# A fused attention and two-layer expert kernel: the matrix engine's order fixed by emission in its middle part, with attention's steps set further apart

## The chip, the cores and the metric

The kernel runs on one core of a Trainium2 chip. A core has five engines with a queue each: TensorE (PE in the profile) for matrix products, VectorE (DVE), ScalarE (ACT), GpSimd (POOL), and SyncE (SP), whose queue here issues every DMA. An engine takes its queue in order; engines wait for each other by semaphores. The metric is the device time of one execution in microseconds, and lower is better.

## The reference

Four batches of eight heads (576 positions, head size 64) go through an attention that adds two parts; its output goes through a gated layer and then a squared-ReLU layer over 2304 tokens.

```
out_d   = softmax(scale * q_d @ k_d.T) @ v_d      # q, k, v averaged over groups of 4 positions
out_loc = softmax(scale * q @ k.T, |i-j| < 4) @ v # a band around the diagonal
x  = repeat(out_d, 4) + out_loc                   # -> (2304, 512)
xn = x / sqrt(mean(x*x) + 1e-6) * rms_g
x  = (silu(xn @ w_gate) * (xn @ w_val)) @ w_out   # 512 -> 1536 -> 512
h  = x @ w_in                                     # 512 -> 2048
out = (s * relu(h)**2 + b) @ w_out2               # 2048 -> 512
```

## The kernel before

Precision comes from splitting each float32 operand into two 16-bit halves and adding three products (high by high, high by low, low by high), so that a product of depth 512 is 12 matmuls in one PSUM tile.

The first layer works on 8 blocks of 288 tokens, two to a batch. `main(blk)` runs `moe1_gv` (12 feature chunks, for each 12 matmuls into `pg`, the gate, and 12 into `pvl`, the value; then the gate's epilogue: tanh on ACT into `u`, two multiplications on DVE, the halves on ACT and POOL) and `moe1_out` (four tiles `po` of 36 matmuls). Both are Python generators that yield after 12 matmuls: this is a **step**. A block has 36 steps. Blocks 0 and 1 run together in `main01`, 48 gate and value steps and then 24 of `po`. `moe1_post` rescales a finished block (its matmuls go into `sn`).

Attention of the next batch is woven in as a side generator, one `next` per step. A batch has four **units** of two heads. Batches 0 and 1 use `early_unit` (float32 transposes on TensorE: tiles `tp`, `tpl`, `tpd`, scores `sl` and `sd`, values `pvd` and `pl`). Batches 2 and 3 use `attn_unit`, whose pieces are, in order:

- load q and k (`qkf`), v (`vd`) and v by windows (`vw`); `vd` and `vw` share one buffer;
- `stats`: squares on ACT, `accb` on POOL, then on TensorE `ss`, from which DVE takes the power of two `sc` to scale by;
- halves of q and k into `qk` (ACT, then DVE), a transposing DMA `qkT<-qk` on SP's queue, and copies into `q_b`;
- `pd` on TensorE from `qk` (the averages), then `qd` and six copies `qd_b`; `sd` on TensorE, softmax, `P_d`, transposing DMA `PdT<-P_d`;
- `sl` on TensorE in two parts, a softmax of each over DVE, ACT and POOL into `P_l`, transposing DMA `PlT<-P_l`;
- halves of the values (`split_v`, on POOL and ACT), then `pvd` and `pl` on TensorE.

`norm` ends a half batch: `ssn`, then `rb` on TensorE. In the kernel before one `yield` stands between two pieces, a unit starts every 10 steps, batch 2 starts with block 2 and batch 3 with block 4. All of this only ranks the instructions: a scheduler with a model of the engines decides at build time in which order each engine's queue holds them, and that order is then fixed on the chip. `tc.high_priority(offset=n)` raises instructions in that ranking.

The weights are fetched and split by another generator, `rest_it` (`prep_gv`, and `weigh` for `w_out`, whose last steps scale the 12 chunks of `w_out`). From block 6 on attention's memory is given to `w_in`, prepared by `prep_in`. The second layer (`ph`, `y`) follows.

Of the kernel before, what the change touches and what calls it, by code (L numbers as in the profile page):

```python
# [8 lines left out]
F32 = mybir.dt.float32  # L9
# [19 lines left out]
GR = 96  # L29
# [3 lines left out]
NJ = 9  # L33
NPART = 4
FP = F1 // NPART
UNIT_STEP = 10
UNIT_STEP0 = 2
UNIT_STEP1 = 4
REST0 = 12
# [32 lines left out]
def kernel(  # L72
# [160 lines left out]
    def load_unit(b, hp, qkf, vd, vw):  # L233
        h0 = 2 * hp
        for t, src in enumerate((q, k)):
            for h in range(2):
                sp.dma_start(out=qkf[:, t, :, h, :], in_=src[b, h0 + h].rearrange("(c p) d -> p c d", p=GR))
        sp.dma_start(out=vd.rearrange("p a r d -> p a (r d)"),
                     in_=v[b, h0:h0 + 2].rearrange("h (t p r) d -> p (h t) (r d)", p=72, r=4))
        sp.dma_start(out=vw[:, :, 0, :], in_=v[b, h0:h0 + 2, 0:WIN, :].rearrange("h p d -> p h d"))  # L240
# [11 lines left out]
        return vs  # L252

    def stats(hp, qkf, vd, junk):
        acc = accs[hp % 2]
        act.activation(out=junk[:, :1536], in_=qkf.rearrange("p t c h d -> p (t c h d)"), func=AF.Square,
                       accum_out=acc[:GR, 0:1])
        act.activation(out=junk[:72, :1024], in_=vd.rearrange("p a r d -> p (a r d)"), func=AF.Square,
                       accum_out=acc[:72, 1:2])
        accb = ap.tile([128, 2], BF16, tag="accb", name="accb")  # L260
        pool.tensor_single_scalar(out=accb, in_=acc, scalar=TINY, op=ALU.add)
        vs = sum4(vd)
        ss = pX.tile([128, 2], F32, tag="x", name="ss")
        pe.matmul(out=ss, lhsT=ones_b, rhs=accb, start=True, stop=True)
        sc, iv = pow2(ap, ss, 2, 13, "sq", 2)
        cs = ap.tile([128, 2], F32, tag="cs", name="cs", bufs=2)
        mul(cs[:, 0:1], iv[:, 0:1], 1.0 / 8, iv[:, 0:1])
        dve.tensor_single_scalar(out=cs[:, 1:2], in_=iv[:, 1:2], scalar=2.0 ** -14, op=ALU.mult)
        return vs, sc, cs

    def softmax_d(sd, scale, de=None):
        dm = ap.tile([128, 3], F32, tag="dm", name="dm", bufs=2)
        dz = ap.tile([128, 3], F32, tag="dz", name="dz", bufs=2)
        dve.tensor_reduce(out=dm, in_=sd, axis=AX.X, op=ALU.max)
        dve.tensor_scalar(out=dm, in0=dm, scalar1=scale, scalar2=-1.0, op0=ALU.mult, op1=ALU.mult)
        if de is None:
            de = ap.tile([128, 3, SD], F32, tag="de", name="de")
        for o in range(3):
            act.activation(out=de[:, o], in_=sd[:, o], func=AF.Exp, bias=dm[:, o:o + 1], scale=scale,
                           accum_out=dz[:, o:o + 1])  # L280
        return de, dz

    def scores_d(qd, cs):
        sd = pX.tile([128, 3, SD], F32, tag="x", name="sd")
# [219 lines left out]
    def attn_unit(b, hp, sq_sum):  # L504
        mp = b <= MASKB
        qkf = ap.tile([GR, 2, 6, 2, D], F32, tag="qkf", name="qkf")
        vd = ap.tile([72, 4, 4, D], F32, tag="vd", name="vd")
        vw = ap.tile([WIN, 2, NJ, D], F32, tag="vd", name="vw")
        load_unit(b, hp, qkf, vd, vw)
        yield  # L510
        qk = ap.tile([GR, 24, 128], F16, tag="qk", name="qk")
        vs, sc, cs = stats(hp, qkf, vd, qk.bitcast(BF16).rearrange("p a b -> p (a b)"))
        yield
        qkv = qkf.rearrange("p t c h d -> p t (c h d)")
        qv = qk.rearrange("p (t l c) x -> p t l (c x)", t=2, l=2)
# [34 lines left out]
        yield  # L550
        for js in JS:
            sl = scores_l([q_b[:, 9 * l:9 * l + 9] for l in range(2)], [kT[:, l] for l in range(2)], js, mp)
            yield
# [6 lines left out]
        sp.dma_start_transpose(out=PlT, in_=P_l.rearrange("p a b -> p (a b)"))  # L560
        vh = ap.tile([WIN, 2, 2, NJ, D], F16, tag="vh", name="vh")
        vdh = ap.tile([72, 2, 4, D], F16, tag="vdh", name="vdh")
        split_v(vs, vw, vdh, vh, sc)
        yield
        od = values_d(vdh, PdT, cs[:, 1:2])
        yield
        for js in JS:
            values_l(b, hp, js, vh, PlT, od, cs[:, 1:2])
            yield
        for hh in range(2):  # L570
            squares(b, hp, hh, sq_sum)
        yield

    def norm(b, hh, sq_sum):
        ss = pX.tile([GR, 3], F32, tag="x", name="ssn")
        for c in range(3):
            cc = 3 * hh + c
# [12 lines left out]
        yield  # L590
        rb = pX.tile([128, TB], F32, tag="x", name="rb")
        for c in range(3):
            for i in range(3):
# [13 lines left out]
        yield  # L607


    ring = [W1[:, 15744 + 1024 * i:15744 + 1024 * i + 1024].bitcast(I32).rearrange("p (n t) -> p n t", t=2)  # L610
# [93 lines left out]
    def moe1_gv(blk, g16, fcs=range(NF1)):  # L704
        for fc in fcs:
# [80 lines left out]

    def attn_batch(b):
        sq_sum = ap.tile([128, S], F32, tag="sqsum", name="sqsum")
        if b == EARLY:
            clear()  # L790
        gens = [(early_unit if b < EARLY else attn_unit)(b, hp, sq_sum) for hp in range(NP)]
        step = UNIT_STEP if b >= EARLY else UNIT_STEP1 if b else UNIT_STEP0
        live = []
        n = halves_ = 0
        while gens or live:
            if gens and n % step == 0:
                live.append(gens.pop(0))
            for g in list(live):
                got = next(g, 0)
                if got == 0:  # L800
                    live.remove(g)
                elif got == "half":
                    halves_ += 1
                    if halves_ == NP:
# [85 lines left out]
    def drain(it):  # L890
        for _ in it:
            pass

    W2 = C2 = None
    for blk in range(NB):
        if blk == NB - 2:
# [30 lines left out]
        for n, ev_ in enumerate(main(blk) if blk else main01()):
            if blk == 0:
                if n % RESTN == 0:
                    for _ in range(REST):  # L930
                        if steps[0] < 12 * NPART + NF1:
                            next(rest_it, None)
            if n == 1 or ev_ == "post":
# [125 lines left out]
```

## Time and profile before

| | |
|---|---|
| median of 3 runs | 1069.01 us (1065.67 to 1071.11) |
| the profiled execution | 1066.8 us, of which the profile's span is 1065.1 us |
| mean granted TensorE clock | 0.971 of full speed |
| busy: TensorE, VectorE, ScalarE, GpSimd | 988.2, 597.1, 517.0, 323.9 us |

Busy time is the time in which an engine has an instruction under way; TensorE's clock has two levels, 1.2 and 2.4 GHz, and a mean of 0.95 over a stretch is a tenth of it at the lower one. In rows of the trace the first number is the start in microseconds from the span's beginning, the second the length, and a bracket at the end gives the time that the engine stood idle just ahead, with what ended it. L716 is line 716 of the kernel.

### The profile page before, as it was taken

The page shows a single profiled execution, that of the slowest core. Times are in us where ns is not written, and L with a number is a line of the kernel's source. Part 1 is how long each engine was busy: PE and PEld are TensorE (multiplying, and loading weights), DVE is VectorE, ACT ScalarE, POOL GpSimd, SP SyncE. Part 2 cuts the span into 40 slices and gives each one's busy share as a digit, 9 for nine tenths or more (in the row PEclk, how much of TensorE's full clock was granted, in tenths as well). Part 3 has the DMA queues.
Part 4 walks back from the last instruction along what each step waited for, and adds up shares of the span by engine and source line. Part 5 has one row for each costly group of instructions (what it writes and reads, how often), then busy time and mean ns, then how long its engine had stood idle before and what let it go on. Part 6 is the DMA issues. An engine that isn't in the chain of part 4 may idle for free.

```text
span 1065.1 us, 20448 instructions
## 1 busy us (share of the span) xinstructions
PE 988.2 (93%) x8198; PEld 668.0 (63%) x8198; DVE 597.1 (56%) x1263; ACT 517.0 (49%) x1174; POOL 323.9 (30%) x417
## 2 busy tenths in 40 slices
PE   7975999999997799888899899999999999999998
PEld 4753777778765677666687677654555545455553
DVE  4798975363884764867826777574332414233240
ACT  3876686355644544555436777663321404132140
POOL 7433753245644355535542206420000000000000
PEclk9986999999988899999999999999999999999999
DMA  9985144010345430555312424300000000000000
GB/s 193 232 223 153 61 134 124 14 24 14 69 83 117 95 62 2 93 103 100 61 24 86 153 86 161 111 1 10 21 10 20 1 30 1 20 11 10 20 1 30
DMA packets 128111, 73.59 MB, mean 69 GB/s; under 512 B 111376, under 2 KB 115984, under 8 KB 128016
## 3 DMA queue, kind: packets, MB, share of 16 engines
q1 hardware_dynamic: 128016, 72.29, 26.9%
q8 instruction: 64, 1.05, 0.4%
q14 instruction: 31, 0.25, 0.1%
HBM read 54.97 MB, written 4.72 MB: 56 GB/s over the span
## 4 chain that ended last, share of the span: by engine, by line
PE 62%; DVE 14%; DMA 12%; ACT 5%; issue 4%; POOL 2%; SPq 1%; DVEq 0%; POOLq 0%; ACTq 0%
PE y L1021 18%; PE ph L1001 17%; PE po L737 8%; PE pg L716 7%; PE pvl L716 6%; DMA stg<-in_moe_w_in_dram 3%; DMA stg<-in_moe_w_out_dram 2%; DMA qkT<-qk 2%; DMA PlT<-P_l 2%; DVE W L638 2%; DVE stg L634 2%; PE pl L369 1%; DMA PdT<-P_d 1%; ACT stg L633 1%; DVE W L130 1%
## 5 line engine op out<-in xcount | busy, mean ns | idle before, releaser
L716 PEld LDWEIGHTS <-W 128*128 128x128 f16 x2304 | 227.5, 100 | 83.9 <-issue 20.7
L1001 PE MATMUL ph<-X,W 128*128 128x384 f16 x1152 | 196.6, 326 | 0.4 <-DVE s4o L681 0.3
L716 PE MATMUL pg<-X,W 128*128 128x288 f16 x1152 | 169.8, 295 | 9.5 <-DVE u L723 8.5
L716 PE MATMUL pvl<-X,W 128*128 128x288 f16 x1152 | 167.8, 292 | 4.8 <-DVE u L192 3.0
L1001 PEld LDWEIGHTS <-W 128*128 128x128 f16 x1152 | 112.6, 98 | 82.7 <-issue 3.3
L1021 PE MATMUL y<-W 128*128 128x512 f16 x648 | 151.6, 379 | 0.0
L737 PEld LDWEIGHTS <-W 128*128 128x128 f16 x1152 | 112.1, 99 | 36.2 <-issue 7.0
L737 PE MATMUL po<-g,W 128*128 128x288 f16 x1008 | 132.5, 289 | 1.0 <-POOL g L727 0.7
L1005 ACT ACTIVATE r<-ph 128x384 f32<-128x384 f32 x96 | 46.9, 489 | 176.1 <-PE ph L1001 126.6
L727 POOL TENSOR_TENSOR g<-u,g 128x288 f16<-128x288 f32 x84 | 73.5, 875 | 136.8 <-ACT g L726 136.8
L1021 PEld LDWEIGHTS <-W 128*128 128x128 f16 x648 | 63.4, 98 | 71.0
L192 DVE SCALAR_TENSOR_TENSOR r<-ph,r 128x384 f32<-128x384 f32 x96 | 53.5, 557 | 59.4 <-ACT r L1005 59.4
L1026 DVE SCALAR_TENSOR_TENSOR ys<-y,ccol,bcol 128x512 f32<-128x512 f32 x18 | 13.5, 751 | 121.1 <-PE y L1021 118.9
L726 ACT ACTIVATE g<-u 128x288 f16<-128x288 f32 x84 | 36.8, 438 | 60.8 <-DVE u L192 59.9
L634 DVE SCALAR_TENSOR_TENSOR stg<-stg 128x512 int32<-128x512 int32 (+1 forms) x53 | 40.3, 760 | 36.4 <-ACT stg L633 36.3
L1009 DVE TENSOR_TENSOR W<-r,W 128x384 f16<-128x384 f32 x72 | 40.1, 558 | 36.5 <-ACT W L1008 36.5
L723 DVE SCALAR_TENSOR_TENSOR u<-u,pvl 128x288 f32<-128x288 f32 x96 | 43.0, 448 | 26.9 <-PE pvl L716 22.2
L1008 ACT ACTIVATE W<-r 128x384 f16<-128x384 f32 x72 | 37.5, 521 | 40.0 <-DVE r L192 40.0
L722 ACT ACTIVATE u<-pg,tsc 128x288 f32<-128x288 f32 x96 | 46.9, 488 | 14.7 <-PE pg L716 13.6
L1021 PE MATMUL y<-W,r2b 128*128 128x512 f16 x216 | 50.0, 379 | 0.0
L192 DVE SCALAR_TENSOR_TENSOR u<-u,pg 128x288 f32<-128x288 f32 x96 | 43.1, 449 | 1.7
L632 ACT ACTIVATE W<-stg 128x512 f32<-128x512 f32 (+1 forms) x53 | 34.0, 644 | 20.3 <-DMA stg<-in_moe_w_out_dram 9.1
(266 smaller groups left out, 1427.1 us busy)
## 6 DMA issues: line engine op xcount, KB each, us to landing
stg<-in_moe_w_out_dram SPq DMA_DIRECT2D x25, 512.0 KB
stg<-in_moe_w_in_dram SPq DMA_DIRECT2D x16, 512.0 KB
out_dram<-ys SPq DMA_DIRECT2D x18, 256.0 KB
W<-in_moe_w_gate_dram SPq DMA_DIRECT2D x10, 384.0 KB
W<-in_moe_w_val_dram SPq DMA_DIRECT2D x10, 384.0 KB
qkf<-in_q_dram SPq DMA_DIRECT2D x26, 144.0 KB
qkf<-in_k_dram SPq DMA_DIRECT2D x26, 144.0 KB
vd<-in_v_dram SPq DMA_DIRECT2D x13, 288.0 KB
```

What stands on the lines that cost most here:

```text
L192: (eng or dve).scalar_tensor_tensor(out=o, in0=a, scalar=s, in1=b, op0=ALU.mult, op1=ALU.mult)
L634: ins = dve.scalar_tensor_tensor(out=stg[:, :, 0], in0=stg[:, :, 1], scalar=-2 ** 31, in1=stg[:, :, 0], op0=ALU.bitwise_and, op1=ALU.bitwi ...
L716: pe.matmul(out=acc, lhsT=Cgv.half(o, FP, lw)[:, f0 * 128:f0 * 128 + 128], rhs=X16[:, kc, 3 * blk:3 * blk + 3, lx, :], start=i == 0, stop= ...
L722: act.activation(out=u, in_=ps[0], func=AF.Tanh, scale=tsc[:, part:part + 1])
L723: dve.scalar_tensor_tensor(out=u, in0=u, scalar=1.0, in1=ps[1], op0=ALU.add, op1=ALU.mult)
L727: pool.tensor_tensor(out=lo, in0=u, in1=hi, op=ALU.subtract)
L737: pe.matmul(out=acc, lhsT=Co.half(fc * 512, 512, lw)[:, m * 128:(m + 1) * 128], rhs=g16(fc)[:, lx, :], start=i == 0, stop=i == 35)
L1001: pe.matmul(out=acc, lhsT=C2.half((p * KC + kc) * 512, 512, lw)[:, f0 * 128:f0 * 128 + 128], rhs=X16[:, kc, 4 * blk:4 * blk + 4, lx, :], s ...
L1005: act.activation(out=r, in_=acc, func=AF.Relu, scale=2.0 ** -23)
L1008: act.activation(out=dst[:, 0, :], in_=r, func=AF.Copy)
L1009: dve.tensor_tensor(out=dst[:, 1, :], in0=r, in1=dst[:, 0, :], op=ALU.subtract)
L1021: pe.matmul(out=y, lhsT=src[:, lx, tt * 128:(tt + 1) * 128], rhs=C3.half(fc * 512, 512, lw), start=i == 0, stop=i == 47)
```

## The change

1. From step 50 of `main01` to the end of block 5 TensorE's queue holds its instructions in the order in which the program emits them (`manual_schedule`); the other engines and the DMAs are still ordered by the scheduler.
2. In `attn_unit` and `norm`, `yield from lag(n)` puts 2 to 6 steps between one piece and the next. Units start every 14 steps, batch 2 starts at step 54 of `main01` (six steps into its `po`) and batch 3 in step 20 of block 3. A unit now takes 32 steps.
3. The windows of v (`vw`) are loaded after the DMA `PlT<-P_l` is issued, no longer with q, k and v.
4. `qk` is made in two pieces (q, then k) instead of one.
5. The three instructions that make `u` are raised by 100 in the ranking.
6. From step 38 of `main01` `rest_it` goes on with the scaling of `w_out`, which stood behind step 48.
7. Batch 1's steps no longer run inside a priority block of their own.

```diff
+ORDERED = 50
+OUT0 = 38
+LAG_SS = 3
+LAG_PD = 6
+LAG_SD = 3
+LAG_SL = 2
+LAG_VH = 3
+LAG_V = 6
+LAG_OD = 2
...
+NORM1 = 56
+START2 = 54
+START3 = 56
...
+    def lag(n):
+
+        for _ in range(n):
+            yield
...
-        vw = ap.tile([WIN, 2, NJ, D], F32, tag="vd", name="vw")
-        load_unit(b, hp, qkf, vd, vw)
-        yield
+        load_unit(b, hp, qkf, vd, None)
+        yield from lag(LAG_SS)
         qk = ap.tile([GR, 24, 128], F16, tag="qk", name="qk")
-        vs, sc, cs = stats(hp, qkf, vd, qk.bitcast(BF16).rearrange("p a b -> p (a b)"))
-        yield
+        vs, sc, cs = yield from stats(hp, qkf, vd, qk.bitcast(BF16).rearrange("p a b -> p (a b)"))
...
-        act.activation(out=qv[:, :, 0], in_=qkv, func=AF.Copy, scale=sc[:GR, 0:1])
-        dve.scalar_tensor_tensor(out=qv[:, :, 1], in0=qkv, scalar=sc[:GR, 0:1], in1=qv[:, :, 0],
-                                 op0=ALU.mult, op1=ALU.subtract)
+        for t in range(2):
+            act.activation(out=qv[:, t, 0], in_=qkv[:, t], func=AF.Copy, scale=sc[:GR, 0:1])
+            dve.scalar_tensor_tensor(out=qv[:, t, 1], in0=qkv[:, t], scalar=sc[:GR, 0:1], in1=qv[:, t, 0],
+                                     op0=ALU.mult, op1=ALU.subtract)
...
         kT = qT[:, 1].rearrange("p (l s) -> p l s", l=2)
-        yield
+        yield from lag(LAG_PD)
         pd = pX.tile([128, 288], F32, tag="x", name="pd")
...
         sp.dma_start_transpose(out=PlT, in_=P_l.rearrange("p a b -> p (a b)"))
+        vw = ap.tile([WIN, 2, NJ, D], F32, tag="vd", name="vw")
+        load_windows(b, hp, vw)
+        yield from lag(LAG_VH)
...
         split_v(vs, vw, vdh, vh, sc)
-        yield
+        yield from lag(LAG_V)
         od = values_d(vdh, PdT, cs[:, 1:2])
-        yield
+        yield from lag(LAG_OD)
...
+            with tc.high_priority(offset=UFIRST):
+                act.activation(out=u, in_=ps[0], func=AF.Tanh, scale=tsc[:, part:part + 1])
+                dve.scalar_tensor_tensor(out=u, in0=u, scalar=1.0, in1=ps[1], op0=ALU.add, op1=ALU.mult)
+                mul(u, u, 2.0 ** -45, ps[0])
...
+            for _ in range(REST):
+                if n >= OUT0 or steps[0] < 12 * NPART + NF1:
+                    next(rest_it, None)
...
+            first = main01()
+            sides.append(attn_batch(1))
+            run_first(first, 0, ORDERED)
+            with tc.manual_schedule(engines={pe.engine}):
+                run_first(first, ORDERED, 1000)
+                for mid in range(2, NB - 2):
+                    middle(mid)
```

The orders of the two built programs show what this moves. First, TensorE's queue in the gate and value steps of blocks 0 and 1, where one unit of batch 1 has its scores (`sl`, `sd`) while the unit ahead of it has its values (`pl`). Before:

```order
L451 MATMUL sl<-qkT_1801 64x70 x10
L369 MATMUL pl<-q_b,qk_1525 64x64
L469 MATMUL sd<-X 64x144
...
L369 MATMUL pl<-q_b,qk_1525 64x64
L469 MATMUL sd<-X 64x144
L369 MATMUL pl<-q_b,qk_1525 64x64 x2
L716 LDWEIGHTS W_86
```

and after the change:

```order
L478 MATMUL sl<-mask,ident_b 64x350
L482 MATMUL sl<-qkT_1801 64x70 x10
L400 MATMUL pl<-q_b,qk_1525 64x64
L500 MATMUL sd<-X 64x144 x6
L400 MATMUL pl<-q_b,qk_1525 64x64 x7
L746 LDWEIGHTS W_86
```

Before, `pl` and `sd` alternate one by one; now they stand in groups, and `tp` with `pvd` likewise. From the first `pg` to the first `po` the queue changes from one tile to another 213 times before and 141 times now. The first matmul that differs is one that the trace of before has at 129.76 us.

Second, TensorE's queue in blocks 2 to 5, from a unit's `ss` on; the lines of dots are matmuls of `pg`, `pvl` or `po`, and the rest of a group. The second unit of batch 2 before, where `pvd` and `pl` belong to the unit ahead:

```order
L264 MATMUL ss<-accb,ones_b 128x2
...
L532 MATMUL pd<-pool_m,qk 128x24
...
L353 MATMUL pvd<-PdT,vdh 64x64
...
L287 MATMUL sd<-qd,qd_b 128x144
...
L369 MATMUL pl<-PlT,vh 64x64
```

and after the change, with the two parts of the scores behind it:

```order
L289 MATMUL ss<-accb,ones_b 128x2
...
L562 MATMUL pd<-pool_m,qk 128x24
...
L384 MATMUL pvd<-PdT,vdh 64x64
...
L317 MATMUL sd<-qd,qd_b 128x144
...
L400 MATMUL pl<-PlT,vh 64x64
...
L332 MATMUL sl<-qkT,q_b 128x70
```

The sequence stays; the number of first-layer matmuls between two groups changes. From `ss` to the main part of `pd` there are 48 here before and 72 now (in the eight units 48 to 60 before, 72 in each now). From `pd` to `sd` there are 26 to 42 before and 36 now. From a unit's `sd` to its `pvd` there are 61 to 98 before and 144 or 156 now. From the end of a unit's scores to its first `pl` there are 119 to 161 before (119 to 133 in six units), and 132 or 144 now, with the next unit's `ss`, `pd` and `sd` and its own `pvd` among them.

Third, SP's queue at the second and third unit of batch 2. Before:

```order
L520 DMA_TRANSPOSE qkT<-qk 128x24x96
L237 DMA qkf<-in_q_dram 96x6x64 x2
L237 DMA qkf<-in_k_dram 96x6x64 x2
L238 DMA vd<-in_v_dram 72x4x256
L240 DMA vw<-in_v_dram 70x2x64
L241 DMA vw<-in_v_dram 70x2x64
L244 DMA vw<-in_v_dram 70x7x64 x2
L549 DMA_TRANSPOSE PdT<-P_d 128x12x128
L520 DMA_TRANSPOSE qkT<-qk 128x24x96
L560 DMA_TRANSPOSE PlT<-P_l 128x18x128
```

and after the change:

```order
L255 DMA qkf<-in_q_dram 96x6x64 x2
L255 DMA qkf<-in_k_dram 96x6x64 x2
L263 DMA vw<-in_v_dram 70x2x64
L578 DMA_TRANSPOSE PdT<-P_d 128x12x128
L264 DMA vw<-in_v_dram 70x2x64
L267 DMA vw<-in_v_dram 70x7x64 x2
L550 DMA_TRANSPOSE qkT<-qk 128x24x96
L588 DMA_TRANSPOSE PlT<-P_l 128x18x128
L255 DMA qkf<-in_q_dram 96x6x64 x2
L255 DMA qkf<-in_k_dram 96x6x64 x2
```

The next unit's `qkT` stands ahead of this unit's `PlT` in both. What moved are the loads: `vd` is no longer queued right behind `qkf` together with `vw` of its own unit, and `vw` now stands around `PdT`.

## Rows read from the trace of the kernel before

**Rows 1.** The page's part 1: busy time of each engine.

```profile
PE 988.2 (93%) x8198; PEld 668.0 (63%) x8198; DVE 597.1 (56%) x1263; ACT 517.0 (49%) x1174; POOL 323.9 (30%) x417
```

**Rows 2.** Busy by stage: length, PE, PEld, DVE, ACT, POOL, granted clock, DMA.

```profile
140.00:217.80 77.80, 77.31 (x710) 57.91 (x708) 40.31 (x95) 45.17 (x119) 26.61 (x34) 0.98 0.33 94
...
262.00:561.60 299.60, 266.72 (x3011) 209.16 (x3009) 194.93 (x457) 149.44 (x347) 148.00 (x173) 0.95 0.37 72
561.60:685.50 123.90, 113.85 (x894) 87.04 (x893) 90.31 (x167) 94.25 (x199) 41.96 (x43) 1.00 0.37 128
```

**Rows 3.** Groups on PE, 262.0 to 561.6 us: busy, mean ns, idle ahead, releaser.

```profile
L716 PE MATMUL pg<-X,W 128*128 128x288 f16 x576 | 85.8, 300 | 6.5 <-DVE u L723 6.5
...
L369 PE MATMUL pl<-PlT,vh 70*64 70x64 f16 x432 | 9.9, 197 | 6.1 <-DMA PlT<-P_l 6.1
L532 PE MATMUL pd<-pool_m,qk 96*128 96x24 f16 x192 | 7.8, 177 | 4.4 <-DVE qk L517 4.2
L353 PE MATMUL pvd<-PdT,vdh 72*64 72x64 f16 (+1 forms) x288 | 6.2, 194 | 5.1 <-DMA PdT<-P_d 4.9
L287 PE MATMUL sd<-qd,qd_b 128*128 128x144 f16 x72 | 6.2, 227 | 3.8 <-DVE qd_b L539 3.8
...
L264 PE MATMUL ss<-accb,ones_b 128*128 128x2 bf16 x8 | 1.3, 168 | 3.0 <-POOL accb L261 3.0
```

**Rows 4.** Timeline of PE in block 3, and one `ss` of batch 3.

```profile
347.76 0.17 PE L264 MATMUL ss<-accb,ones_b 128*128 128x2 bf16 x1
347.79 1.63 PE L716 MATMUL pvl<-X,W 128*128 128x288 f16 x12
349.25 1.63 PE L716 MATMUL pg<-X,W 128*128 128x288 f16 x12
...
358.66 0.79 PE L532 MATMUL pd<-pool_m,qk 96*128 96x24 f16 x23 [3.67 <-DVE qk L517]
...
368.29 0.66 PE L369 MATMUL pl<-PlT,vh 70*64 70x64 f16 x30 [2.13 <-DMA PlT<-P_l]
...
476.34 0.18 PE L264 MATMUL ss<-accb,ones_b 128*128 128x2 bf16 x1
```

**Rows 5.** Timeline of SP's queue at the same two places.

```profile
358.66 2.93 SPq L520 DMA_TRANSPOSE qkT<-qk  x1
361.69 2.74 SPq L560 DMA_TRANSPOSE PlT<-P_l  x1
...
480.87 3.65 SPq L520 DMA_TRANSPOSE qkT<-qk  x1
```

**Rows 6.** Timeline of PE: tiles alternating and in groups, batch 1.

```profile
173.94 0.45 PE L353 MATMUL pvd<-P_d,vs 72*64 72x64 f32 x8
174.42 0.44 PE L432 MATMUL tp<-ident_f,qkf 96*128 96x96 f32 x3
...
177.39 0.25 PE L432 MATMUL tp<-ident_f,qkf 96*128 96x96 f32 x1
...
179.91 0.29 PE L353 MATMUL pvd<-P_d,vs 72*64 72x16 f32 x2
...
187.79 0.33 PE L369 MATMUL pl<-q_b,qk 70*64 70x64 f32 x2
...
191.88 0.48 PE L369 MATMUL pl<-q_b,qk 70*64 70x64 f32 x4
...
217.22 0.69 PE L369 MATMUL pl<-PlT,vh 70*64 70x64 f32 x16
...
219.41 0.95 PE L469 MATMUL sd<-X 64*64 64x144 f32 x12
```

**Rows 7.** Timeline of DVE: the low half of `P_l`, twice.

```profile
293.09 2.44 DVE L557 TENSOR_TENSOR P_l<-ch,P_l 128x350 f16<-128x350 f32 x1
...
318.32 1.41 DVE L557 TENSOR_TENSOR P_l<-ch,P_l 128x350 f16<-128x350 f32 x2
```

**Rows 8.** Timeline of POOL beside the first of these.

```profile
293.05 2.10 POOL L132 TENSOR_TENSOR vw<-vw,sqs 70x1152 f32<-70x1152 f32 x1
```

More of the change, by code (lines that the diff above doesn't have):

```diff
@@ L35 @@
 FP = F1 // NPART
-UNIT_STEP = 10
+UNIT_STEP = 14
+FLOATS = 4
+HALF0 = 20
+HALF_STEP = 12
+ORDERED = 50
+OUT0 = 38
+UFIRST = 100
+LAG_SS = 3
[5 more added lines that the diff above has]
+LAG_OD = 2
+LAG_RB = 3
+LAG_X = 2
+NORM1 = 56
+START2 = 54
+START3 = 56
 UNIT_STEP0 = 2
@@ L307 @@
     last = []
+    normed = set()
     gates = {}
@@ L563, in attn_unit, with norm @@
         split_v(vs, vw, vdh, vh, sc)
-        yield
+        yield from lag(LAG_V)
         od = values_d(vdh, PdT, cs[:, 1:2])
-        yield
-        for js in JS:
+        yield from lag(LAG_OD)
+        for hh, js in enumerate(JS):
             values_l(b, hp, js, vh, PlT, od, cs[:, 1:2])
-            yield
-        for hh in range(2):
             squares(b, hp, hh, sq_sum)
-        yield
-    def norm(b, hh, sq_sum):
+            yield ("half", None)[hh]
+    def norm(b, hh, sq_sum, l1=1, l2=1):
         ss = pX.tile([GR, 3], F32, tag="x", name="ssn")
@@ L589, in norm @@
                 pool.tensor_tensor(out=r, in0=r, in1=rp[i], op=ALU.subtract)
-        yield
+        yield from lag(l1)
         rb = pX.tile([128, TB], F32, tag="x", name="rb")
@@ L606, in norm @@
             gates[3] = tuple(last)
-        yield
+        yield from lag(l2)
+        normed.add((b, hh))
     ring = [W1[:, 15744 + 1024 * i:15744 + 1024 * i + 1024].bitcast(I32).rearrange("p (n t) -> p n t", t=2)
@@ L788, in attn_batch @@
         sq_sum = ap.tile([128, S], F32, tag="sqsum", name="sqsum")
[L789 to L792, printed above, removed]
+        floats = FLOATS if b else NP
+        gens = [early_unit(b, hp, sq_sum) if hp < floats else attn_unit(b, hp, sq_sum) for hp in range(NP)]
+        starts = [HALF0 + HALF_STEP * (hp - floats) if hp >= floats else hp * (UNIT_STEP1 if b else UNIT_STEP0)
+                  for hp in range(NP)]
         live = []
@@ L795, in attn_batch @@
         while gens or live:
-            if gens and n % step == 0:
+            if gens and n >= starts[NP - len(gens)]:
+                if b and NP - len(gens) == floats:
+                    clear()
                 live.append(gens.pop(0))
@@ L804, in attn_batch, with attn_later, later_norm @@
                     if halves_ == NP:
-                        live.append(norm(b, 0, sq_sum))
+                        live.append(later_norm(b, 0, sq_sum) if b else norm(b, 0, sq_sum))
             n += 1
             yield
-        if b >= EARLY:
-            yield from norm(b, 0, sq_sum)
-        yield from norm(b, 1, sq_sum)
+        yield from later_norm(b, 1, sq_sum) if b else norm(b, 1, sq_sum)
+    def attn_later(b):
+        sq_sum = ap.tile([128, S], F32, tag="sqsum", name="sqsum")
+        if b == EARLY and FLOATS == NP:
+            clear()
+        gens = [attn_unit(b, hp, sq_sum) for hp in range(NP)]
+        live = []
+        n = halves_ = 0
+        while gens or live:
+            if gens and n % UNIT_STEP == 0:
+                live.append(gens.pop(0))
+            for g in list(live):
+                got = next(g, 0)
+                if got == 0:
+                    live.remove(g)
+                elif got == "half":
+                    halves_ += 1
+                    if halves_ == NP:
+                        live.append(later_norm(b, 0, sq_sum))
+            n += 1
+            yield
+        yield from later_norm(b, 1, sq_sum)
+    def later_norm(b, hh, sq_sum):
+        yield
+        while b == 1 and now[0] < NORM1:
+            yield
+        yield from norm(b, hh, sq_sum, LAG_RB, LAG_X)
     def rest():
@@ L892, in drain, with tick, run_first, middle @@
             pass
+    sides = []
+    now = [0]
+    def tick():
+        now[0] += 1
+        for g in list(sides):
+            if next(g, 0) == 0:
+                sides.remove(g)
+    def run_first(it, n0, n1):
+        for n in range(n0, n1):
+            ev_ = next(it, 0)
+            if ev_ == 0:
+                return
+            for _ in range(REST):
+                if n >= OUT0 or steps[0] < 12 * NPART + NF1:
+                    next(rest_it, None)
+            if ev_ == "post":
+                run_posts()
+            if n == START2:
+                sides.append(attn_later(2))
+            tick()
+    def middle(blk):
+        while (blk // 2, blk % 2) not in normed:
+            tick()
+        for n, _ in enumerate(main(blk)):
+            if n == 2:
+                run_posts()
+            if 36 * (blk - 2) + n == START3:
+                sides.append(attn_later(3))
+            tick()
+        if blk == NB - 3:
+            while sides:
+                tick()
     W2 = C2 = None
@@ L922 @@
             side = prep_in()
-        elif blk % 2 == 0 and blk // 2 + 1 < B:
-            side = attn_batch(blk // 2 + 1)
-        if blk == 1:
+        if 0 < blk < NB - 2:
             continue
[L927 to L933, printed above, removed]
+        if blk == 0:
+            first = main01()
[5 more added lines that the diff above has]
+                    middle(mid)
+            continue
+        for n, ev_ in enumerate(main(blk)):
+            if n == 1:
                 run_posts()
             if side is not None:
-                with tc.high_priority(offset=SIDE0 if blk == 0 else SIDE):
+                with tc.high_priority(offset=SIDE):
                     next(side, None)
-        if (blk == 0 or blk % 2 == 1) and side is not None:
+        if blk % 2 == 1 and side is not None:
             drain(side)
```

12 lines of the change are left out of this document (7 added, 5 removed).

## The prediction

> **What bounds the kernel now.** I read the page's busy times first. TensorE is busy for 988.2 of 1065.1 us, the next engine for little over half [rows 1]: the time can change only where TensorE stands still, runs at its lower clock, or takes longer over the same matmuls. The busy times by stage say where that is [rows 2]. In the gate and value steps of blocks 0 and 1 (140 to 217.8 us) it stands still for 0.5 us: there only cheaper matmuls can help. In blocks 2 to 5 (262 to 561.6 us) it is busy for 266.72 of 299.60 us: 32.9 us of waiting. The clock's mean there is 0.95, so a tenth of the stretch ran at 1.2 instead of 2.4 GHz, and 5% of 299.6, that is 15.0 us of work, was lost. This stage can give back 32.9 + 15.0 = 47.9 us at most. In blocks 6 and 7 10.05 us are idle at full clock.
>
> The groups of PE in blocks 2 to 5 tell what the waits are for [rows 3]: `pl` 6.1 us for the transposing DMA of `P_l`, `pvd` 5.1 for that of `P_d`, `pd` 4.4 for `qk`, `sd` 3.8 for `qd_b`, `ss` 3.0 for `accb`; and the gate `pg` 6.5 for the DVE instruction that frees its PSUM tile. All but the last are of one kind: a consumer stands in TensorE's order too few matmuls behind its producer. The timeline shows one such unit whole [rows 4]: `ss` at 347.76, `pd` only at 358.66 after 3.67 us of idling, `pl` after 2.13 more. SP's queue beside it [rows 5]: the next unit's `qkT` starts when `qk` is ready, and this unit's `PlT` stands behind it.
>
> **The change part by part.** *The lags.* A step is 12 matmuls, and one follows the other after 349.25 - 347.79 = 1.46 us [rows 4], so 0.122 us a matmul. By the orders, `ss` to `pd` grows from 48 matmuls (5.9 us) to 72 (8.8 us). What it must cover ran from 10.9 us (347.76 to 358.66, where `pd` waited) down to 4.5 us (`ss` at 476.34, `qkT` starting at 480.87) [rows 4, 5]: at the long end 2.1 us of waiting stay, below 8.8 none. `sd` to `pvd` grows by 46 matmuls or more, 5.6 us, beyond any wait that its 5.1 us in all can hold per unit: gone. `ss` to `sd` grows by about 25 matmuls, 3.1 us, against 3.8 us for all eight units: nearly gone. Scores to `pl` changes least: from about 128 to 144 matmuls, 17.6 us, and with the other unit's `pd`, `sd` and the `pvd` in between (7.8 + 6.2 + 6.2 us busy over eight units, 2.5 us each, of which I count 2) [rows 3] 19.6 us. What it must cover: 24 matmuls to the next `ss` (2.9 us), `ss` to `qk` (4.5 to 10.9), 3.0 us of issuing `qkT` ahead of it (358.66 to 361.69) and 6.6 from there to the `pl` that waited (361.69 to 368.29) [rows 4, 5]: 17.0 to 23.4 us. So `pl` waits for 0 to 3.8 us a unit, less what `pd` has waited already. The waits that are not the gate's are 32.9 - 6.5 = 26.4 us; I leave 5.0 of them, which is about half a microsecond in each unit and 1 us for the start of a batch. The chain's lengths lie between the two ends, and with units 14 steps apart instead of 10 fewer instructions of another unit stand in DVE's and ACT's queues; that is why I take a value near the short end.
>
> *The windows of v.* `vw` held the buffer in which the next unit's `vd` lands; the `ss` wait (3.0 us) [rows 3] is of that kind, and goes. The same four DMAs are issued, now around `PdT`, and delay what stands behind them in SP's queue, the next `qkT`; `split_v`, which reads them, is three steps (4.4 us) behind. *The two pieces of `qk`* are eight more instructions on DVE and eight on ACT, which are busy for 194.93 and 149.44 of 299.60 us [rows 2]: no cost, and a shorter way to `pd`. *The gate's epilogue first*: of 6.5 us [rows 3] I leave 5.0, since the order in DVE's queue is decided at build time, and an instruction ahead that waits for a DMA holds `u` up all the same. *`w_out` in step 38* moves its scaling into a stretch where DVE is busy for 40.31 and ACT for 45.17 of 77.80 us [rows 2]. It fits; no gain. If it didn't, the epilogue of the gate would be late there, and TensorE with it.
>
> *The clock.* 15.0 us lost for 32.9 us of waits is 0.46 us for each. With 10.0 us of waits left 4.6 are lost. So blocks 2 to 5 give 47.9 - 14.6 = 33.3 us.
>
> *The grouping in blocks 0 and 1* is what the orders show beside the table of lags. Alternating, 16 `pl` and 12 `sd` took from 187.79 to 191.88 + 0.48, so 4.57 us; in groups 0.69 + 0.95 = 1.64 [rows 6]. Eleven changes of tile too many cost 2.93 us, 0.27 each. Six `tp` and twelve `pvd` took from 177.39 to 179.91 + 0.29, so 2.81 us; in groups, from three `tp` in 0.44 and eight `pvd` in 0.45, it is 0.88 + 0.68 = 1.56 [rows 6]: ten changes cost 1.25, 0.125 each. There are 72 changes fewer, worth 9.0 us at the one price and 19.4 at the other. About 22 are of the dear kind (5.9 us) and 50 of the cheap one (6.3); I take 11, since a few stand ahead of 140 us, where TensorE is not the bound. TensorE has nothing else to wait for there, so this comes off the path whole.
>
> *DVE and POOL.* One `P_l` instruction took 2.44 us on DVE while POOL multiplied `vw` for 2.10 us; two such took 1.41 together elsewhere [rows 7, 8]. So 1.7 us were added by the neighbour. The Trainium skill (SBUF — State Buffer, Who interferes with whom) explains it: a DVE instruction with two SBUF inputs and a GpSimd instruction that reads SBUF need one shared pair of ports, and whichever starts second waits for the whole of the other. By that rule the sixteen half-size `qk` instructions, each with two such inputs, offer twice the occasions, which would speak against the change; the trace agrees with the rule in this row. By the rows alone such delays are already within the 4.5 to 10.9 us above, and I add nothing.
>
> *Blocks 6 and 7* keep their side work; I take 0, from -4 to +3 us, as its matmuls for `w_in` come a little earlier in the order.
>
> **The sum.** 1066.8 (the profiled execution) - 33.3 - 11 = 1022.5 us. The median of the runs shown lies 2.2 us above that execution: 1024.7.
>
> **The rivals.** *Grouping gives nothing* because the vectors' work, not TensorE, then sets the pace of blocks 0 and 1. For it: with 11 us less in 77.8, DVE and ACT are still under 70% busy [rows 2], so little; against it the 0.5 us of idling now. 1035.7 us.
>
> *DVE and POOL shut each other out in every unit*: POOL's `vw` multiplication meets the `qk` pieces, and each unit pays 2.1 us [rows 8] on the way from `ss` to `pl`: 8 x 2.1 = 17 us more, 1041.7. Rows 7 show the price once; the orders put the two near each other.
>
> *The chain is long in half of the units*: four wait for 3.8 us, with the gate's 6.5 and 3 for the starts 25 us; times 1.46, 36.5 us lost, so 11.4 gained: 1066.8 - 11 - 11.4 + 2.2 = 1046.6. For it: the 10.9 us of block 3. *In all of them*: 8 x 3.8 + 6.5 = 36.9, times 1.46 is 53.9, 6.0 more than now: 1064.0, which a measurement hardly tells from no change (the runs of before spread by 0.5%, 5.4 us, and that is the bound that I use).
>
> *Slower*: SP's queue. `PlT` waits behind the next unit's `qkT`, and now `vw` is in front of that as well, at a place where TensorE's order allows no other work to be pulled in. If this takes `PlT` 5.5 us beyond its 19.6 in every unit, 8 x 5.5 + 6.5 = 50.5, times 1.46 is 73.7 us, 25.8 more than now, and less 11: 1066.8 + 2.2 + 14.8 = 1083.8. It decides from (47.9 + 11) / 1.46 = 40.3 us of waits on, which is 4.2 us a unit beside the gate's. Against it: the long end of the chain gives 3.8.
>
> **How the numbers follow.** The forecast has a chance of 0.53, grouping without effect 0.10, the ports 0.10, half of the units long 0.14, all long 0.05, slower 0.08. The predicted time is the forecast's, 1025. Its best end is 3 us of waits left (4.4 with the clock) and 19.4 for grouping: 1066.8 - 43.5 - 19.4 + 2.2 = 1006.1. The range goes from there to 1054, past the half-long case and short of the all-long one; outside lie the slower case, the all-long one and a few hundredths at either end, together 0.2. Faster by over 0.5% is below 1063.7: 0.53 + 0.10 + 0.10 and 0.12 of the half-long case, 0.85. Slower is 0.08, and 0.07 remain within.
>
> **What would show it.** In the profile after, blocks 0 and 1 should end some 11 us earlier with no new idle time of TensorE, and `tp`, `pvd`, `pl`, `sd` stand in groups. Blocks 2 to 5 should take about 266 us, with a clock of 0.98 or more; of the waits `pvd` on `PdT` should be gone, and `pd` and `pl` have less than 1 us a unit. The prediction is wrong if `pl` or `pd` waits for over 2 us in most units, if the gate's wait grows well past 6.5 us because DVE's queue is blocked at `q_b`, or if the second layer is not left as it is.

## The result, and the profile after

The changed kernel takes 1056.99 us (median of 4 runs, 1055.88 to 1061.04); the kernel before 1070.06 beside it. The ratio is 0.988 (0.985 to 0.991), so it is faster by 1.2%, under a third of what was forecast (1025, range 1006 to 1054). The profiled execution took 1061.04 us (span 1059.3), the slowest of the four; it stands 5.8 us below that of before, while the medians differ by 13.1. So stages are compared with each other below, and whole kernels by medians. A stage comes from one execution: blocks 6 and 7, for one, took 123.9 us here and 127.2 in a run whose edit does not touch them (experiment 3, before), so differences of 2 or 3 us say little.

The page's part 1:

```profile
PE 976.0 (92%) x8197; PEld 661.2 (62%) x8198; DVE 595.9 (56%) x1271; ACT 518.1 (49%) x1182; POOL 326.1 (31%) x417
```

TensorE does the same matmuls in 12.2 us less than in [rows 1], but stands still for 6.4 us more (83.3 after 76.9). By stage, with the columns of [rows 2]: gate and value steps of blocks 0 and 1 from 140 us on, their `po`, blocks 2 to 5, blocks 6 and 7.

```profile
140.00:207.60 67.60, 64.90 (x670) 51.09 (x668) 46.09 (x105) 50.33 (x128) 26.03 (x33) 0.95 0.39 110
207.60:265.80 58.20, 52.49 (x533) 40.55 (x531) 25.07 (x66) 29.01 (x72) 29.83 (x43) 0.94 0.17 38
265.80:555.80 290.00, 257.15 (x2948) 202.61 (x2948) 188.12 (x441) 143.37 (x337) 140.03 (x167) 0.96 0.35 69
555.80:679.70 123.90, 113.80 (x892) 87.00 (x892) 87.25 (x164) 92.59 (x196) 43.62 (x40) 1.00 0.38 128
```

The second line's counterpart in the kernel before:

```profile
217.80:262.00 44.20, 44.20 (x435) 35.25 (x432) 20.20 (x46) 24.66 (x58) 20.30 (x30) 1.00 0.05 11
```

The first stage ends 10.2 us earlier (207.6 after 217.8), though its clock is lower and TensorE waits for 2.7 us in it. The second, which had no idle time, is 14.0 us longer: 5.7 us of that is waiting, 3.5 the clock (0.94 of 58.2 us), and the rest about a hundred matmuls that moved into it with the start of batch 2. Blocks 2 to 5 are 9.6 us shorter, all of it busy time: the clock, 63 matmuls that moved forward, and fewer changes from one tile to another (240 in the trace of before, 188 now). Second and third together take 348.2 us after 343.8 before. The forecast saw 33.3 us go in blocks 2 to 5; in place of that these two stages grew by 4.4. Blocks 6 and 7 and the second layer are as they were.

In blocks 2 to 5 TensorE idles for 32.85 us, as before (32.88). But the groups show other waits than [rows 3]:

```profile
L746 PE MATMUL pg<-X,W 128*128 128x288 f16 x576 | 81.5, 293 | 16.0 <-DVE u L754 15.9
L746 PE MATMUL pvl<-X,W 128*128 128x288 f16 x576 | 79.9, 289 | 7.2 <-DVE u L754 4.9 <-DVE u L210 2.4
L768 PE MATMUL po<-g,W 128*128 128x288 f16 x576 | 75.3, 289 | 3.5 <-DVE u L754 3.5
L400 PE MATMUL pl<-PlT,vh 70*64 70x64 f16 x432 | 10.1, 200 | 5.9 <-DVE poi L206 5.9
...
L384 PE MATMUL pvd<-PdT,vdh 72*64 72x64 f16 (+1 forms) x288 | 5.9, 191 | 0.0
L562 PE MATMUL pd<-pool_m,qk 96*128 96x24 f16 x168 | 5.4, 175 | 0.0
L317 PE MATMUL sd<-qd,qd_b 128*128 128x144 f16 x63 | 5.1, 226 | 0.0
```

No attention group waits for its own producer any more: not for `PdT`, `PlT`, `qk` or `qd_b`. All but 0.2 us are now waits for an instruction late in DVE's queue, `u` above all: its two instructions on DVE read the PSUM tiles of value and gate, and free them for the next `pg`, `pvl` or `po`. What DVE itself waited for in blocks 2 to 5 (us in total, times, longest), after the change and then before:

```profile
DVE dz L319 <- ACT de L304: 20.3, 7, 6.5
DVE u L754 <- PE pvl L746: 16.3, 11, 2.8
DVE q_b L554 <- DMA qkT<-qk: 14.5, 6, 3.4
```

```profile
DVE xn L600 <- PE rb L594: 26.8, 5, 5.7
DVE X L374 <- PE pl L369: 21.1, 12, 3.0
DVE q_b L524 <- DMA qkT<-qk: 12.2, 7, 2.9
...
DVE dz L289 <- ACT de L279: 3.3, 3, 1.4
```

Before, DVE mostly waited for TensorE. Now `dz`, which takes the sums of the exponentials `de`, holds its queue for 20.3 us. The timeline at the longest of these waits, in block 3 (SP, ACT, DVE, PE):

```profile
340.99 2.78 SPq L588 DMA_TRANSPOSE PlT<-P_l  x1
343.95 0.43 SPq L263 DMA_DIRECT2D vw<-in_v_dram  x1
...
346.85 1.00 SPq L255 DMA_DIRECT2D qkf<-in_q_dram  x2
...
351.79 1.48 ACT L280 ACTIVATE qk<-qkf 96x1536 bf16<-96x1536 f32 x1 [7.65 <-DMA qkf<-in_k_dram]
...
355.08 0.17 DVE L319 TENSOR_SCALAR dz<-dz 128x3 f32<-128x3 f32 x1 [6.53 <-ACT de L304]
355.16 0.55 DVE L405 SCALAR_TENSOR_TENSOR X<-pl,cs,od 128x320 f32<-128x320 f32 x1
...
355.76 0.48 PE L400 MATMUL pl<-PlT,vh 70*64 70x64 f16 x10 [5.91 <-DVE poi L206]
```

Read it from the end: `pl` waits for DVE, whose `X` reads the tile of the `pl` before; `X` stands behind `dz`; `dz` needs `de` on ACT; ACT stands at the squares of the *next* unit's q and k, which wait for a load issued behind `PlT` and `vw`. The scores `sd`, from which `de` is made, had been computed from 344.99 us on. A second kind of delay, near the end of block 4 (DVE, POOL, PE):

```profile
457.33 4.85 DVE L547 SCALAR_TENSOR_TENSOR qk<-qkf,sqs,qk 96x768 f16<-96x768 f32 x2
...
458.30 3.07 POOL L152 TENSOR_TENSOR vh<-vw,vh 70x1152 f16<-70x1152 f32 x1
...
463.08 0.44 DVE L754 SCALAR_TENSOR_TENSOR u<-u,pvl 128x288 f32<-128x288 f32 x1
463.57 0.65 PE L768 MATMUL po<-g,W 128*128 128x288 f16 x4 [3.51 <-DVE u L754]
```

Two `qk` instructions, which take 1.0 us each at their shortest, take 4.85 beside POOL's work on the windows, and `u` stands behind them.

### The profile page after: what moved, and what is told of

It is laid out like the page before. It is cut to its first block, busy times and chain, and to the rows that moved or that the text cites. A ratio compares the mean times of both kernels' runs of the same rounds, so it can differ in the third digit from the quotient of the medians.

```text
span 1059.3 us, 20473 instructions
## 1 busy us (share of the span) xinstructions
PE 976.0 (92%) x8197; PEld 661.2 (62%) x8198; DVE 595.9 (56%) x1271; ACT 518.1 (49%) x1182; POOL 326.1 (31%) x417
## 4 chain that ended last, share of the span: by engine, by line
PE 41%; DMA 5%; DVE 4%; ACT 3%; issue 1%; POOL 0%; SPq 0%; POOLq 0%; DVEq 0%; ACTq 0%
PE y L1120 18%; PE ph L1100 17%; DMA stg<-in_moe_w_in_dram 2%; PE pvl L746 2%; DMA stg<-in_moe_w_out_dram 2%; PE pg L746 2%; PE po L768 1%; DVE W L668 1%; DVE stg L664 1%; ACT stg L663 1%; ACT W L662 1%; DMA qkT<-qk 0%; DVE W L148 0%; DMA vw<-in_v_dram 0%; ACT W L147 0%
## 5 line engine op out<-in xcount | busy, mean ns | idle before, releaser
L746 PE MATMUL pvl<-X,W 128*128 128x288 f16 x1152 | 164.9, 291 | 9.6 <-DVE u L754 4.9
L664 DVE SCALAR_TENSOR_TENSOR stg<-stg 128x512 int32<-128x512 int32 (+1 forms) x53 | 36.6, 690 | 33.7 <-ACT stg L663 33.6
```

Source lines behind the costliest of these rows:

```text
L664: ins = dve.scalar_tensor_tensor(out=stg[:, :, 0], in0=stg[:, :, 1], scalar=-2 ** 31, in1=stg[:, :, 0], op0=ALU.bitwise_and, op1=ALU.bitwi ...
L746: pe.matmul(out=acc, lhsT=Cgv.half(o, FP, lw)[:, f0 * 128:f0 * 128 + 128], rhs=X16[:, kc, 3 * blk:3 * blk + 3, lx, :], start=i == 0, stop= ...
```

## The experiments

Main theory: the waits that the lags were meant for are gone, and delays in DVE's queue took their place; theory B blames `dz`, theory A the neighbour on POOL. The rival, theory C, is the fixed order of TensorE itself.

**1. The squares behind the exponentials.**

`exps[0]` is the last `de` of the unit ahead, and `squared` holds the two squares of `stats`.

```diff
...
+        with tc.issue_after(exps[0]):
+            squared(acc, qkf, vd, junk)
...
```

> The changed kernel with ScalarE's squares of the next unit's q, k and v queued behind the exponentials of the unit ahead, so that these no longer stand behind squares that wait for a load. Theory B: VectorE's idle time ahead of dz falls from 20 us to under 8, the one wait of 5.9 us of pl in block 3 goes, TensorE idles about 10 us less in blocks 2 to 5, and the time falls by 8 to 14 us to 1043 to 1049. Theory A: dz moves as told, but the time falls by 3 us at most, since the next delay in VectorE's queue takes its place.

1046.34 us, ratio 0.974 (0.970 to 0.979) to before, so 10.6 us below the changed kernel. Blocks 2 to 5 take 275.9 us, 14.1 less, and TensorE idles for 20.4 us in them, 12.5 less. DVE's wait at `dz` there:

```profile
DVE dz L326 <- ACT de L310: 4.7, 5, 1.6
```

The wait in block 3 is gone. This order of two kinds of ACT instructions cost nearly as much as the whole change gained. Of TensorE's waits `pg` keeps its own:

```profile
L753 PE MATMUL pg<-X,W 128*128 128x288 f16 x577 | 82.9, 296 | 16.2 <-DVE u L761 15.5 <-DVE u L210 0.6
L753 PE MATMUL pvl<-X,W 128*128 128x288 f16 x576 | 80.1, 290 | 0.4 <-DVE u L761 0.4
```

**2. The same in the kernel before.**

> The kernel before with the squares behind the exponentials alone. Theory B says that dz holding VectorE's queue is a wait which the change made (3.3 us of VectorE's idle time there before, 20.3 after): within 4 us of 1070. If 10 us come off here too, this wait cost as much before and the change is not what made it.

1080.94 us, ratio 1.009 (1.006 to 1.012): slower, which neither expectation has. It is not for waits: TensorE waits longer for `PlT` (9.6 us) and `qd_b` (7.5) than in [rows 3], but in all it idles for 30.4 us in blocks 2 to 5, less than before. What grew there is its busy time, 277.4 us after 266.7. Nearly half of that is the clock (0.93 after 0.95); the rest is in two groups, which took 9.9 and 6.2 us in [rows 3]:

```profile
L376 PE MATMUL pl<-PlT,vh 70*64 70x64 f16 x432 | 16.1, 203 | 9.6 <-DMA PlT<-P_l 9.6
L294 PE MATMUL sd<-qd,qd_b 128*128 128x144 f16 x72 | 12.3, 262 | 7.5 <-DVE qd_b L546 7.5
```

In this kernel the scheduler also orders TensorE, and with the edit it has `pl` and `sd` alternate in some units. By the traces TensorE changes from one tile to another 313 times in blocks 2 to 5 here, 305 times with experiment 3's edit and 321 with experiment 5's, after 240 without an edit; with the fixed order it is 188 (193 in experiment 7). So this run does not price the squares' order in the kernel before. That the change made the long wait rests on DVE's waits above: 3.3 us at `dz` before, 20.3 after.

**3. The windows of v off POOL**, in both kernels.

The scaling of the windows and their halves move to ACT and DVE.

```diff
-        halves(vhv[:, 0], vhv[:, 1], vw.rearrange("p h j d -> p (h j d)"), sc[:WIN, 1:2], pool)
+        halves(vhv[:, 0], vhv[:, 1], vw.rearrange("p h j d -> p (h j d)"), sc[:WIN, 1:2], dve)
```

> The changed kernel with the windows of v scaled and halved by ScalarE and VectorE instead of GpSimd. Theory A (TensorE's waits for u come from VectorE instructions that GpSimd's two long instructions on the windows stretch): in blocks 2 to 5 the excess length of VectorE instructions beside these two, 26 us, goes, for some 10 us of new VectorE work; TensorE's idle time there falls from 33 us to 14 to 20, and the time by 13 to 25 us against the changed kernel's 1057. Theory B (the waits come from dz, which holds VectorE's queue until ScalarE's exponentials are done): at most 5 us. Theory C (the fixed order alone costs it, since TensorE can take nothing else): within 5 us.

> The same edit in the kernel before. Theory A, in which VectorE's delays were covered there by TensorE's waits for attention: 0 to 10 us less than 1070, clearly less than the edit gives in the changed kernel. If the same 13 to 25 us come off, the delays cost as much before, and they are not what took the gain away.

After: 1053.35 us, ratio 0.982 (0.979 to 0.986). Before: 1058.63 us, ratio 0.987 (0.984 to 0.990), which is 12 us from its 1070.88. Theory A fell as put: it asked for 13 to 25 us in the changed kernel and got 3.6, and the delay beside POOL costs the kernel before more than the changed one, so it was no cover that the change took away. It is real all the same: blocks 2 to 5 took 280.1 and 286.1 us with this edit, 10 and 14 less than without it.

**4. Both mends together.**

> The changed kernel with both edits: the squares behind the exponentials, and the windows of v on ScalarE and VectorE. In blocks 2 to 5 the one edit alone gave 14.1 us and the other 10.0. If they take away different delays of u: blocks 2 to 5 take 264 to 270 us, the time is 1037 to 1043. If u is late for the same reason in both (one delay in VectorE's queue hides the other): 273 to 276 us in blocks 2 to 5, and 1045 to 1050.

1036.36 us, ratio 0.968 (0.965 to 0.971). `po` of blocks 0 and 1, then blocks 2 to 5:

```profile
205.80:265.10 59.30, 52.44 (x533) 40.34 (x532) 25.87 (x70) 28.52 (x73) 26.33 (x41) 0.94 0.15 32
265.10:528.10 263.00, 250.38 (x2949) 199.68 (x2948) 172.93 (x445) 143.62 (x337) 112.00 (x154) 1.00 0.40 77
```

Blocks 2 to 5 are down to 263.0 us at full clock, with 12.6 us idle, and `pg` waits for 6.9:

```profile
L753 PE MATMUL pg<-X,W 128*128 128x288 f16 x577 | 78.7, 286 | 6.9 <-DVE u L761 6.5 <-DVE u L210 0.3
L753 PE MATMUL pvl<-X,W 128*128 128x288 f16 x576 | 78.5, 286 | 1.1 <-DVE u L210 1.1
L775 PE MATMUL po<-g,W 128*128 128x288 f16 x576 | 74.2, 286 | 2.1 <-ACT g L764 1.5 <-POOL g L765 0.5
```

The two gains add (by the ratios 1.4% and 0.6%, together 2.0%), and this version is faster than both kernels. Against the kernel before the two stages still give back only 21.5 us (343.8 to 322.3).

**5. Grouping alone, and the change without it.** In the kernel before, `nullcontext()` in place of batch 1's priority block; in the changed kernel, the block put back:

```diff
-            if next(g, 0) == 0:
+            with tc.high_priority(offset=SIDE0) if now[0] <= ORDERED else nullcontext():
+                got = next(g, 0)
+            if got == 0:
```

> The kernel before with nothing changed but that batch 1's steps run without a priority block of their own, which puts tp, pvd, pl and sd in groups (144 changes of tile from the first pg to the first po, 213 before). If the term of the prediction is right: the gate and value steps of blocks 0 and 1 are 9 to 14 us shorter, and the time 1056 to 1061. If VectorE or ScalarE set the pace there: within 4 us of 1070, with new idle time of TensorE in these steps.

> The changed kernel with batch 1's steps back in a priority block of their own until step 50 (200 changes of tile from the first pg to the first po, 141 without it). If grouping is worth what it gave alone: 9 to 15 us more than 1057, in the gate and value steps of blocks 0 and 1. If it was worth that only in the kernel before: under 4 us more.

Alone: 1056.09 us, ratio 0.984 (0.981 to 0.988), as fast as the whole change. Its gate and value steps from 140 us on:

```profile
140.00:207.70 67.70, 64.81 (x708) 51.12 (x706) 43.01 (x96) 44.84 (x120) 26.67 (x34) 0.97 0.42 108
```

The stage is 10.1 us shorter than in [rows 2]: practically the same matmuls keep TensorE busy for 12.5 us less, and 2.4 us of new idle time stand against that. Blocks 2 to 5 are 2.3 us shorter. Without the grouping the changed kernel takes 1078.58, ratio 1.009 (1.006 to 1.012): slower than before, 21.6 us above the change, more than either expectation. By the profiles its gate and value steps take 75.3 us (67.6 in the changed kernel) and the `po` stage 68.9 (58.2), where 45 more matmuls stand, more tiles alternate too, and the clock is lower (0.90 after 0.94). Equal groups of 36 matmuls in the gate and value steps: without the grouping (first fence, 140 to 215 us), and in the changed kernel (140 to 207.6 us).

```profile
L400 PE MATMUL pl<-q_b,qk 70*64 70x64 f32 x36 | 4.6, 249 | 0.0
...
L482 PE MATMUL sl<-qkT 64*64 64x70 f32 x36 | 2.6, 227 | 0.0
```

```profile
L400 PE MATMUL pl<-q_b,qk 70*64 70x64 f32 x36 | 1.8, 229 | 0.0
...
L482 PE MATMUL sl<-qkT 64*64 64x70 f32 x36 | 1.4, 220 | 0.0
```

The mean duration of one hardly differs; what they keep TensorE busy for together does. That is why it shows neither as idle time nor in the mean. The tiles that alternate here differ in shape (the first pair of numbers behind the names, 70*64 or 64*64). The few rows of the kernel before in which two tiles of one shape alternate don't show the loss:

```profile
154.68 0.27 PE L451 MATMUL sl<-P_l 64*64 64x70 f32 x1
154.68 0.33 PE L469 MATMUL sd<-X 64*64 64x144 f32 x1
154.79 0.22 PE L451 MATMUL sl<-P_l 64*64 64x70 f32 x1
154.86 0.28 PE L469 MATMUL sd<-X 64*64 64x144 f32 x1
```

These four start within 0.18 us; 16 `pl` of 70*64 alternating with 12 `sd` of 64*64 took 4.57 us [rows 6], 0.16 each. No run tests the shape by itself.

**6. TensorE's order free**, `nullcontext()` in place of `manual_schedule`.

> The changed kernel without the fixed order of TensorE from step 50 on: the scheduler orders it too. Theory C (the fixed order alone costs the gain): 5 to 15 us less than 1057. Theory B (VectorE's and ScalarE's queues are the cause, and these the scheduler orders in both): within 5 us of 1057, with waits for u as before.

> The changed kernel with both edits and without the fixed order of TensorE. If the fixed order costs what it cost alone (5.6 us, most of it in the po stage of blocks 0 and 1, which took 45 us without it and 58 with it): 1028 to 1033. If the fixed order is what lets the lags work once the queues of ScalarE and VectorE are mended: 1038 to 1050, with waits of pd, pvd and sl for their producers in blocks 2 to 5, as in the changed kernel without the fixed order.

Without the mends 1051.41 us, ratio 0.982 (0.979 to 0.985), 5.6 less, at the edge of what can be told apart (the changed kernel's interval begins at 0.985). With them 1035.85, ratio 0.971 (0.968 to 0.975): the same as experiment 4, and between the two expectations. `po` of blocks 0 and 1 then takes 45.0 us and blocks 2 to 5 277.3, together 322.3, again as there. TensorE idles for 19.5 us in the two stages in both, 6.9 and 12.6 in experiment 4, none and 19.5 here. So the fixed order moves work and waits into the `po` stage, and costs something only while the queues beside it are late. Theory C is a small part.

**7. Batch 2 six steps later** (`START2 = 60`, `START3 = 62`), without and with the mends.

> The changed kernel with batches 2 and 3 started six steps later (step 60 of main01, step 26 of block 3). Theory: the 14.3 us that the po stage of blocks 0 and 1 grew by are mostly new losses (5.7 us idle, 4 at the lower clock), since the first unit of batch 2 meets the norms of batch 1 there; pd waits for xn, which stands behind q_b and its DMA in VectorE's queue. Then the po stage takes 46 to 51 us instead of 58.2, blocks 2 to 5 grow by 2 to 4 us of moved matmuls, and the time falls by 3 to 9 us to 1048 to 1054. If the growth is only work that was moved forward: the total stays within 3 us of 1057.

> The changed kernel with both mends and batches 2 and 3 six steps later. If the po stage's waits (6.9 us idle, 2.6 of it pd for xn) are a loss of their own: 1027 to 1032 against 1036.4. If they only move, as they did without the mends (1058.4 against 1057): 1034 to 1039.

1058.41 and 1037.66 us, ratios 0.989 (0.986 to 0.992) and 0.969 (0.965 to 0.973): no gain. The `po` stage fell to 53 us in both, and the total stayed. My reading that its waits were a loss of that place was wrong: a later start takes them along.

**8. Three small parts undone**: `vw` loaded with q, k and v again; `qk` whole; `UFIRST = 0`.

> The changed kernel with the windows of v loaded with q, k and v again, ahead of the unit's own transposes. If the moved loads make the squares late: the wait of 5.9 us in block 3, where four of them stand ahead of the next unit's q and k, goes, VectorE's idle time ahead of dz falls from 20 to 12 or less, and the time falls by 4 to 10 us against 1057. If the squares' place ahead of the exponentials is enough by itself: dz still waits for 15 us or more in all, and the time is within 4 us of 1057 or above it (the loads then hold up the next unit's v).

> The changed kernel with qk in one piece again. The prediction costed the two pieces at nothing: within 3 us of 1057. If each piece is caught by GpSimd's windows anew: 3 to 10 us less.

> The changed kernel without the raised priority of the three instructions that make u. The prediction gave it 1.5 us. If it holds the waits for u down: 3 to 15 us more than 1057, with the waits of pg and pvl for u above the 23 us that they sum to. If the order in which VectorE's queue is built has little to do with it, since the delays come from loads and neighbours that the scheduler doesn't foresee: within 3 us.

`vw` early: 1071.27 us, ratio 1.001 (0.998 to 1.004), the whole gain gone. The wait of 5.9 us in block 3 does go, and `dz` waits for 12.5 us in place of 20.3 (between the two expectations), but `ss` takes over in blocks 2 to 5:

```profile
PE ss L289 <- POOL accb L285: 24.0, 4, 8.0
```

`accb` needs the squares of `vd`, whose buffer the `vw` of the unit ahead now holds. The moved loads are thus a needed part, and make one long wait of `dz`; the rest of the wait at `dz` is there without them. `qk` whole: 1058.94, ratio 0.990 (0.985 to 0.995); `UFIRST = 0`: 1057.79, 0.990 (0.988 to 0.993). Neither part does anything measurable.

**9. Grouping and the windows off POOL in the kernel before**, no lags.

> The kernel before with the grouping and the windows of v on ScalarE and VectorE, so without lags, fixed order and the rest of the change. The two gave 14.8 and 12.2 us alone: 1041 to 1047 if they add. Against the changed kernel with both edits (1036.4) it tells what lags and fixed order are worth once VectorE's queue is mended: 5 to 11 us by this, of the 33 that the prediction gave them; nothing if it comes to 1037 or less.

1043.28 us, ratio 0.977 (0.975 to 0.980). Against 1036.36: lags, loads, fixed order and the mend of the squares together are worth 7 us by the medians, 10 by the ratios. Without that mend (1053.35, experiment 3) they cost 10 by the medians, 5 by the ratios.

## Why the prediction was wrong

- **The clock and the waits as the place of the gain**: right. Only waits, the clock and what matmuls cost moved the time; the second layer and blocks 6 and 7 stayed. The price of 0.46 us of clock for each of waiting did not hold: the changed kernel lost 11.6 us (0.96 of 290.0) beside 32.9 of waits, and with both mends blocks 2 to 5 lost none beside 12.6.
- **The grouping**: right in kind, and in size for its stage. I took 11 us of 9.0 to 19.4; the stage gave 10.1 alone and 10.2 in the change. The whole kernel gave 14.8 alone and 21.6 inside the change, where all the gain is its. The 12.5 us of busy time for 63 changes of tile fewer from 140 us on (150 to 87 in the traces) are 0.20 each, between my two prices. Against "no new idle time" stand 2.4 to 2.7 us of it.
- **The lags**: each wait that they were to remove is gone, more fully than I put it (I left 5.0 us). For `ss` that hangs on the moved loads (experiment 8). No run takes the lags alone.
- **The step that failed** is "blocks 2 to 5 give 47.9 - 14.6 = 33.3", and in it "of 6.5 us [rows 3] I leave 5.0" for the gate. The waits for `u` were 8.5 us before, since `pvl` had 2.0 that I counted among those to go (the line behind this list). They became 26.7 us (`pg`, `pvl` and `po`), and 5.9 of `pl` came on top, all on DVE's queue: 32.85 us of waits instead of the 10.0 that I left. I followed every producer to its consumer on TensorE, but asked of DVE's and ACT's queues little more than how busy they were (194.93 and 149.44 of 299.60 us). I did write that an instruction ahead which waits "holds `u` up all the same", and followed none. An instruction that waits in an in-order queue is not busy, and holds all behind it, as `dz` did for 6.53 us in block 3. I named "DVE's queue is blocked at `q_b`" as what would make me wrong; it was blocked at `dz` as well, through ACT and a load two queues away. With both delays mended the `po` stage and blocks 2 to 5 gave 21.5.
- **The early start of batch 2** I had not priced: the `po` stage, without idle time before, grew by 14.0 us, of which 5.7 are waits and 3.5 the clock. By experiments 6 and 7 these are moved there rather than made there.
- **`vw`, `qk`, `w_out`, `u`**: `qk` cost nothing, as put; `u` gave nothing that can be measured, where I had put 1.5 us. `vw` was mis-sized: I gave its move 3.0 us, and undoing it costs 14. `w_out` was not tried alone.
- **The rivals**: "DVE and POOL shut each other out" names a real delay, worth 12 us in the kernel before, but puts it on the way from `ss` to `pl`; in block 4 it strikes `u`. The Trainium skill (SBUF — State Buffer, Who interferes with whom) has a DVE instruction with two SBUF inputs contend with a GpSimd instruction that reads SBUF; the trace agrees at 457.33 us, where two `qk` took 4.85 us beside POOL's `vh` of 3.07.

```profile
L716 PE MATMUL pvl<-X,W 128*128 128x288 f16 x576 | 84.1, 295 | 2.0 <-DVE u L192 2.0
```

What stays open: some 12 of the 33 us also after both mends. TensorE then idles for 12.6 us in blocks 2 to 5, some 8 of it in `pg` and `pvl` for `u`, and for 6.9 in the `po` stage; which instruction ahead of `u` each is due to was not tested. Nor was it tested why the scheduler's order of the kernel before alternates more in blocks 2 to 5 with each edit; what an edit gives in the kernel before holds that too.

## What to carry to other kernels

When a wait is taken from the engine that sets the pace, follow the queues of the engines that feed it: for each buffer that this engine needs back, list what stands ahead of the freeing instruction, and what each of these waits for, across ACT and the loads too. A change of many parts should be taken apart before it is believed: here one side effect, the order of a few small matmuls, carried the gain, and the rest, which was the point, cost time until two delays in the queues beside TensorE were mended. Busy time can hold a loss as well: compare what equal groups of matmuls take together.

## What the runs showed of the hardware

Alternating small float32 matmuls between two tiles of different shape stretched a group 1.9 to 2.6 times (2.6 us for 1.4, 4.6 for 1.8) with TensorE counted as busy throughout; in the kernel of experiment 2, where only some units alternate, the float16 groups `pl` and `sd` of blocks 2 to 5 grew 1.6 and 2.0 times (16.1 us for 9.9, 12.3 for 6.2). And a VectorE instruction that is held by GpSimd's need not be large: one of 128x5 elements took 2.39 us at 268.88 us, where POOL's `vh` ran from 268.86 for 2.38; another of the same form takes 0.17.

```profile
268.88 2.39 DVE L361 TENSOR_SCALAR z<-z 128x5 f32<-128x5 f32 x1
...
299.72 0.17 DVE L361 TENSOR_SCALAR z<-z 128x5 f32<-128x5 f32 x1
```

```profile
268.86 2.38 POOL L152 TENSOR_TENSOR vh<-vw,vh 70x1152 f16<-70x1152 f32 x1 [3.95 <-ACT vh L151]
```
